# Attention's probabilities times values: one float32 product per block in place of three float16 products

## The chip, the cores and the metric

One core of a Trainium2 chip runs the kernel. The metric is device time in microseconds (us) of one execution; the time before is the median of three runs. The engines are PE (TensorE: matrix products, with its weight loads listed apart as PEld), DVE (VectorE), ACT (ScalarE), POOL (GpSimd) and SP (SyncE, which here issues all DMAs). Stationary operands are loaded by a weight load, moving operands stream past them, and sums are kept in PSUM banks.

## The reference

Three layers follow one another. Shapes: batch 4, heads 8, sequence 576, head size 64; the second layer has width 512 and 2048; the third has eight experts of 512 and 1024.

```python
scores = scale * np.matmul(q, k.transpose(0, 1, 3, 2))
scores = np.where(causal, -1e9, scores + np.minimum(bias, 0.0))   # bias from cumulated s
attn = np.exp(scores - max);  attn = attn / (sum + 1e-09)
x = np.matmul(attn, v)                       # -> (2304 tokens, 512)
h = x @ w_in;  g = h * sigmoid(1.702 * h);  x = g @ w_out
P = balanced(exp(x @ w_gate))                # eight rounds of row and column sums
out = sum_e P[:, e] * (relu(x @ w1[e]) @ w2[e])
```

## The kernel before, in words

**Stages.** Attention and the first feed-forward layer (`hp`, `acc`) are interleaved; then the last two token blocks of that layer go through in one wide pass (`accw`); then come the eight experts (`h..`, `y`). The change touches attention alone.

**The planner.** The program is put in order when it is built. `Sequencer` keeps a planned time for each engine, with rough costs per instruction (line 117). Instructions for DVE, ACT, POOL and SP are held and issued by planned time and by rank (0 goes first, then 1, 2, 3); PE's go out at once. The main loop (line 1587) asks at each step which kind of PE work is ready, in this order: V's scale, transposing finished tokens, values, transposing probabilities, scores, and last the feed-forward layer. `any_copy` (line 410) puts a copy on DVE or on ACT, whichever has the smaller planned load, `any_less` (line 417) a subtraction on POOL unless DVE is ahead by 3000 planned ns.

**Attention.** A batch and a range of queries make a group: queries 0 to 255 (two blocks of 128) or 256 to 575 (two blocks of 128 and one of 64). With 8 heads and 4 batches there are 64 entries in `heads`, and each runs as units: one unit of two query blocks, or three units of one block. That makes 128 units, and 480 blocks of 128 keys by 128 or 64 queries. A unit goes through `scores` (products into bank `sp`, mask and maximum on DVE, exponent on ACT, result `sm`), `turn` (line 791: transposes `sm` into bank `tp`, splits the result into the float16 pair `ph`, scaled by 2^15, and `pl`), `values` (line 811) and, per head, `finish` (line 833: the sum of the probabilities stands in a 65th column; DVE divides). Values of a head gather in one bank, `op`, which `finish` empties before the next head's values begin.

**V before.** The largest value of V per head is found (`find_vmax`, `find_vpow`: DMA `vr`, reduction `vmax`, a transpose `vtp`, a power of two `vw`, `vd`, a small float32 product `vbp`, copy `vpow`), V is scaled by it and split into a float16 pair (`prep_v`; both halves show as `v` in the trace; from the second batch on V comes again by DMA as `va`). A block of values is three products: `ph` by V's high half, `ph` by its low half, `pl` by its high half. `finish` takes the scale out again.

**The weights of the first layer** come as 64-bit words in 32 chunks (`conv_load`, `conv`, line 455). DVE decodes a chunk in four passes (`t`), ACT and POOL split it into a float32r pair (`wih`, `wil`, `woh`, `wol`). These have rank 2, so attention's instructions go first. Chunks from number 16 on need room that attention's first batch occupies: line 1086 waits for its last heads, and line 1066 for V of the second batch. The feed-forward layer runs over token blocks of 256; it holds two blocks at a time, starts with blocks 0 and 1 as far as weight pairs are converted, and a block's buffer comes free only when the block has gone through all eight pairs. Finished tokens of attention wait for such a buffer.

Of the kernel before, what the change touches and what calls it, by code (L numbers as in the profile page):

```python
# [23 lines left out]
PSCALE = 2.0**15  # L24
# [11 lines left out]
NEXT_V = 11  # L36
# [262 lines left out]
def kernel(  # L299
# [16 lines left out]
    BH = B * H  # L316
# [295 lines left out]

    def load_v(n):
        if n >= len(heads):
            return
        b, h, _, _, _, nkb, _ = extent(n)
        if n < 2 * H:
            h0 = h // 3 * 3
            va_of[n] = vraw[0, h // 3][:, h - h0].rearrange("p (a d) -> p a d", d=D)[:, 0:nkb]
            return  # L620
        va = apool.tile([128, nkb, D], F32, tag="va", name="va", bufs=2)
        nc.sync.dma_start(out=va, in_=vP[b, h, :, 0:nkb])
        va_of[n] = va

    v0s = [apool.tile([128, 5, D + 1], F16, name=f"v0{i}") for i in range(2)]
    v1s = [apool.tile([128, 5, D], F16, name=f"v1{i}") for i in range(2)]
    vmax = apool.tile([128, BH], F32, name="vmax")
    vpow = apool.tile([128, 2, BH], F32, name="vpow")  # L630
    ones_b = apool.tile([H, 128], F32, name="ones_b")
    vraw = {}

    def find_vmax(b, i):

        h0, h1 = 3 * i, min(H, 3 * i + 3)
        if b == 0:
            x = spool.tile([128, (h1 - h0) * 5 * D], F32, name=f"vr{i}")
        else:
            x = mpool.tile([128, (h1 - h0) * 5 * D], F32, tag="st", name="vr", bufs=2)  # L640
        x = x.rearrange("p (h a) -> p h a", h=h1 - h0)
        nc.sync.dma_start(out=x, in_=vP[b, h0:h1].rearrange("h p a d -> p h (a d)"))
        vraw[b, i] = x
        cols = slice(b * H + h0, b * H + h1)
        nc.vector.tensor_reduce(out=vmax[:, cols], in_=x, axis=AX.X, op=ALU.max, apply_absolute_value=True)

    scaled = set()

    def find_vpow(b, i0, i1):

        h0, h1 = 3 * i0, min(H, 3 * i1)
        n, cols = h1 - h0, slice(b * H + h0, b * H + h1)
        for i in range(i0, i1):
            find_vmax(b, i)
        w = apool.tile([H, 4], F32, tag="vw", name="vw", bufs=2)
        dg = apool.tile([H, 2, H], F32, tag="vd", name="vd", bufs=2)
        yield vmax
        tp = bank("T", [128, 512], "vtp")
        nc.tensor.transpose(tp[:n, 0:128], vmax[:, cols], ident)
        nc.vector.tensor_reduce(out=w[:n, 0:1], in_=tp[:n, 0:128], axis=AX.X, op=ALU.max)  # L660
        nc.vector.tensor_scalar(out=w[:n, 1:2], in0=w[:n, 0:1], scalar1=2.0**-100, scalar2=None, op0=ALU.max)
        i = w.bitcast(I32)
        nc.vector.tensor_scalar(
            out=i[:n, 2:3], in0=i[:n, 1:2], scalar1=0x7F800000, scalar2=0x7F800000,
            op0=ALU.bitwise_and, op1=ALU.bitwise_xor,
        )
        nc.vector.tensor_scalar(
            out=i[:n, 3:4], in0=i[:n, 1:2], scalar1=0x7F800000, scalar2=None, op0=ALU.bitwise_and
        )
        for m, c in ((0, 2.0**13), (1, 2.0**-14)):  # L670
            nc.vector.tensor_scalar(
                out=dg[:n, m, 0:n], in0=ident[:n, :n], scalar1=w[:n, 2 + m:3 + m], scalar2=c,
                op0=ALU.mult, op1=ALU.mult,
            )
        yield dg
        bp = bank("T", [128, 512], "vbp")[:, 0:2 * n].rearrange("p (m n) -> p m n", m=2)
        nc.tensor.matmul(bp, lhsT=ones_b[:n], rhs=dg[:n, :, 0:n], start=True, stop=True)
        nc.vector.tensor_copy(vpow[:, :, cols], bp)
        if b == 0:
            for i in range(i0, i1):  # L680
                x = vraw[b, i]
                r = vpow[:, 0, 3 * i:3 * i + x.shape[1]].rearrange("p (h o) -> p h o", o=1)
                nc.gpsimd.tensor_tensor(out=x, in0=x, in1=r.to_broadcast(list(x.shape)), op=ALU.mult)
        scaled.update((b, h) for h in range(h0, h1))

    vpows = []

    def begin_vpow(b, i0, i1, rank):
        seq.rank = rank
        g = find_vpow(b, i0, i1)  # L690
        vpows.append((g, next(g)))
        seq.rank = 0
# [12 lines left out]
    n_pv = 0  # L705
    due = []

    def more_vpow():

        if due and not any(in_mpool(c) for c in range(n_conv, n_load)):  # L710
            begin_vpow(due.pop(0), 0, 3, 1)

    def more_v():

        nonlocal n_pv
        seq.rank = 1 if n_v else 0
        while n_pv < min(len(heads), (units[n_v][0] if n_v < NU else 0) + 2):
            b, h = extent(n_pv)[0:2]
            if (b, h) not in scaled:
                break  # L720
            if n_pv not in va_of:
                load_v(n_pv)
            prep_v(n_pv)
            n_pv += 1
            load_v(n_pv)
        seq.rank = 0

    def prep_v(n):
        if n >= len(heads):
            return  # L730
        b, h, _, _, _, nkb, _ = extent(n)
        va = va_of.pop(n)
        v0, v1 = v0s[n % 2][:, 0:nkb], v1s[n % 2][:, 0:nkb]
        if n >= 2 * H:
            r = vpow[:, 0, b * H + h:b * H + h + 1]
            if seq.load("DVE") <= seq.load("ACT"):
                nc.vector.tensor_scalar(out=va, in0=va, scalar1=r, scalar2=None, op0=ALU.mult)
            else:
                nc.scalar.activation(out=va, in_=va, func=ACTF.Copy, scale=r)
        any_copy(v0[:, :, 0:D], va)  # L740
        any_less(v1, va, v0[:, :, 0:D])
        v3_of[n] = (v0, v1)
# [48 lines left out]
    def turn(i):  # L791
        sm, blocks = live[i]
        tp = bank("T", [128, 512], "tp")
        at, spots = 0, []
        for qb, rows, ke, a in blocks:
            for kb in range(qb + 1):
                nc.tensor.transpose(
                    tp[:, at:at + rows], sm[:rows, a + kb * 128:a + kb * 128 + 128], ident[:rows, :rows]
                )
                spots.append((qb, kb, rows, at))  # L800
                at += rows
        ph = apool.tile([128, 512], F16, tag="ph", name="ph", bufs=2)
        pl = apool.tile([128, 512], F16, tag="pl", name="pl", bufs=2)
        nc.scalar.activation(out=ph[:, 0:at], in_=tp[:, 0:at], func=ACTF.Copy, scale=PSCALE)
        nc.vector.scalar_tensor_tensor(
            out=pl[:, 0:at], in0=tp[:, 0:at], scalar=PSCALE, in1=ph[:, 0:at],
            op0=ALU.mult, op1=ALU.subtract,
        )
        live[i] = (ph, pl, blocks, spots)

    def values(i):
        n, u = units[i]
        qb0 = extent(n)[6][0]
        v3 = v3_of[n]
        ph, pl, blocks, spots = live.pop(i)
# [5 lines left out]
        for m, (qb, rows, ke, a) in enumerate(blocks):  # L821
            mine = [x for x in spots if x[0] == qb]
            o = op[:rows, qb - qb0, :]
            for w, (_, kb, _, at) in enumerate(mine):
                for part, nv in ((ph, 2), (pl, 1)):
                    for j in range(nv):
                        v = v3[j][:, kb, :]
                        nc.tensor.matmul(
                            o[:, 0:v.shape[1]], lhsT=part[:, at:at + rows], rhs=v,
                            start=(w == 0 and part is ph and j == 0),  # L830
                            stop=(w == len(mine) - 1 and part is pl and j == nv - 1),
                        )
    def finish(n):
# [11 lines left out]
        for _, r, c0, c1 in parts:  # L845
            nc.vector.tensor_scalar(
                out=den[:r, c0:c1], in0=op[:r, c0:c1, D], scalar1=1.0e-9 * PSCALE, scalar2=None, op0=ALU.add
# [3 lines left out]
        at = b * H + h  # L851
        for xt, r, c0, c1 in parts:
            nc.vector.scalar_tensor_tensor(
                out=xt[:r, :, h * D:(h + 1) * D], in0=op[:r, c0:c1, 0:D], scalar=vpow[:r, 1, at:at + 1],
                in1=den[:r, c0:c1].rearrange("p (a o) -> p a o", o=1).to_broadcast([r, c1 - c0, D]),
                op0=ALU.mult, op1=ALU.mult,
            )
        v3_of.pop(n)
# [45 lines left out]
    def can_value():  # L904
        if n_v >= n_t or units[n_v][0] not in v3_of:
            return never
# [3 lines left out]
        x = [live[n_v][0], live[n_v][1], *v3_of[n]]  # L910
        return max([seq.slot(ps_a, "O") if n not in outs else 0] + [seq.settled(a.tensor.name) for a in x])

    def do_value():
# [4 lines left out]
        if i in ends:  # L918
            seq.rank = 1
            n = ends[i]  # L920
            if n % (2 * H) == NEXT_V and n // (2 * H) + 1 < B:
                due.append(n // (2 * H) + 1)
            seq.rank = 0
# [139 lines left out]
    def way(c):  # L1063

        if in_mpool(c):
            if c < 4 * NP1 and (1, 0) not in vraw:
                return None, 0, 0
# [5 lines left out]
    def convert():  # L1073
# [12 lines left out]
        if c == 4 * NP0 and stage[0] is spool:  # L1086
            if n_s < NU and units[n_s][0] < 2 * H - 2 or n_v < NU and units[n_v][0] < 2 * H - 2:
                return
            if min(n_pv, n_prep) < 2 * H or spool.held() or spool2[0].held():
                return  # L1090
# [346 lines left out]
    begin_vpow(0, 0, 1, 0)  # L1437
    load_qk(2)
    nc.gpsimd.memset(ones_b, 1.0)
    for v0 in v0s:  # L1440
        nc.gpsimd.memset(v0[:, :, D:D + 1], 1.0)
# [5 lines left out]
    begin_vpow(0, 1, 3, 1)  # L1447
# [139 lines left out]
    while moe1_can is not None:  # L1587
# [3 lines left out]
        more_vpow()  # L1591
# [205 lines left out]
```

## Time and profile before

| | us |
|---|---|
| median of 3 runs | 2116.03 |
| lowest and highest | 2112.77, 2116.62 |
| profiled execution, span from first to last instruction | 2111.7 |
| PE busy | 2042.9 |
| PEld busy | 1315.4 |
| DVE busy | 1281.5 |
| ACT busy | 755.5 |
| POOL busy | 361.5 |

The profile gives the span of one execution; the median of the runs lies 4.3 us above it, which is what lies around the span and what differs between runs. Busy time is the time in which an engine has an instruction in work. Products on PE overlap, and a product's length is its way through the array; how fast products follow one another is read from their starts. The chain of waits follows the last instruction back to what released it; its shares say what the time was waiting for. Granted clock 1.00 is the upper of PE's two levels (2.4 GHz).

### The profile page before, as it was taken

How to read it: one execution, taken by the hardware profiler on the slowest of the kernel's cores; microseconds unless marked ns; L12 is line 12 of the kernel's file. 1: busy time of each engine (PE TensorE's matmuls, PEld its weight loads, DVE VectorE, ACT ScalarE, POOL GpSimd, SP SyncE). 2: the span in 40 equal slices, each digit the busy share in tenths (PEclk: the TensorE clock that was granted, in tenths of full speed). 3: DMA queues.
4: the chain of work that ended last, by engine and by line, in shares of the span. 5: the costliest groups of instructions: out<-in, count | busy, mean ns of one | idle time of the engine just before them, and what ended most of it. 6: DMA issues, size and time to landing. Idle time of an engine off the chain costs nothing.

```text
span 2111.7 us, 33686 instructions
## 1 busy us (share of the span) xinstructions
PE 2042.9 (97%) x13186; PEld 1315.4 (62%) x13186; DVE 1281.5 (61%) x2823; ACT 755.5 (36%) x1478; POOL 361.5 (17%) x363
## 2 busy tenths in 40 slices
PE   5888999999999999999999999999999999999999
PEld 3688899999987555455555555555555555555554
DVE  8999765653547754765755565565466566646333
ACT  5765564654534433312323222221232322222111
POOL 7567344443344300000000000000000000000000
PEclk9989999999999999999999999999999999999999
DMA  6354343331135642333323222123232322211220
GB/s 215 114 152 141 108 128 92 96 87 54 41 83 173 190 132 72 108 109 119 101 100 120 73 74 104 70 103 130 88 102 98 120 73 96 95 58 68 83 83 31
DMA packets 132931, 215.43 MB, mean 102 GB/s; under 512 B 14628, under 2 KB 78692, under 8 KB 132772
## 3 DMA queue, kind: packets, MB, share of 16 engines
q1 hardware_dynamic: 132772, 213.28, 31.3%
q8 instruction: 104, 1.70, 0.4%
q14 instruction: 55, 0.45, 0.1%
HBM read 190.41 MB, written 18.29 MB: 99 GB/s over the span
## 4 chain that ended last, share of the span: by engine, by line
PE 86%; DVE 8%; issue 2%; DMA 1%; ACT 1%; POOL 1%; SPq 0%; DVEq 0%; ACTq 0%; POOLq 0%
PE y L257 35%; PE hD L257 9%; PE hA L257 8%; PE hp L257 7%; PE acc L257 5%; PE hC L257 4%; PE hB L257 4%; PE hE L257 4%; DVE t L257 4%; PE sp L257 2%; PE tp L257 2%; PE op L257 2%; PE accw L257 1%; DVE sm L257 1%; DVE pl L257 1%
## 5 line engine op out<-in xcount | busy, mean ns | idle before, releaser
L257 PE MATMUL y<-w2o,h 128*128 128x512 f16 x3456 | 751.7, 379 | 0.0
L257 PEld LDWEIGHTS <-h 128*128 128x128 f16 x3456 | 337.6, 98 | 402.6
L257 PEld LDWEIGHTS <-w1o 128*128 128x128 f16 x4032 | 394.3, 98 | 268.0 <-issue 4.9
L257 DVE SCALAR_TENSOR_TENSOR acc<-y,pq,acc 128x512 f32<-128x512 f32 x126 | 94.6, 751 | 347.6 <-PE y L257 347.1
L257 PE MATMUL hD<-xt,w1o 128*128 128x384 f16 x1152 | 218.7, 326 | 3.7 <-DVE c L257 3.2
L257 PE MATMUL hA<-xt,w1o 128*128 128x384 f16 x1152 | 218.6, 326 | 0.0
L257 ACT ACTIVATE m<-hA 128x384 f32<-128x384 f32 x96 | 46.0, 480 | 408.0 <-PE hA L257 407.1
L257 PE MATMUL hp<-xh,wih 128*128 128x256 f32 (+1 forms) x512 | 154.5, 302 | 3.5 <-ACT wih L257 3.1
L257 PE MATMUL hp<-xh,wil 128*128 128x256 f32 (+1 forms) x512 | 152.3, 297 | 0.2 <-DVE wil L257 0.2
L257 PE MATMUL hp<-xl,wih 128*128 128x256 f32 (+1 forms) x512 | 152.2, 297 | 0.0
L257 ACT ACTIVATE c<-hA 128x384 f32<-128x384 f32 x96 | 47.1, 491 | 291.7 <-PE hA L257 291.5
L257 POOL TENSOR_TENSOR gl<-t,gh 128x512 fp32r<-128x512 f32 x70 | 94.1, 1345 | 163.8 <-ACT gh L257 139.8
L257 ACT ACTIVATE sm<-sm,stats 64x576 f32<-64x576 f32 (+4 forms) x160 | 93.7, 602 | 56.4 <-DVE stats L257 56.0
L257 DVE SCALAR_TENSOR_TENSOR u<-hE,u 128x384 f32<-128x384 f32 x96 | 53.5, 557 | 96.8 <-PE hE L257 96.6
L257 PE MATMUL acc<-gh,woh 128*128 128x256 f32 x384 | 111.1, 289 | 0.0
L257 PE MATMUL hE<-xt,w1o 128*128 128x384 f16 x576 | 109.4, 326 | 0.3 <-DVE sc L257 0.3
L257 PE MATMUL hB<-xt,w1o 128*128 128x384 f16 x576 | 109.3, 326 | 0.0
L257 PE MATMUL hC<-xt,w1o 128*128 128x384 f16 x576 | 109.3, 326 | 0.0
L257 PE MATMUL acc<-gl,woh 128*128 128x256 f32 x384 | 108.5, 282 | 0.0
L257 PE MATMUL acc<-gh,wol 128*128 128x256 f32 x384 | 108.3, 282 | 0.0
L257 DVE SCALAR_TENSOR_TENSOR t<-t,hp 128x512 f32<-128x512 f32 x72 | 49.1, 682 | 92.8 <-ACT t L257 92.8
L257 DVE SCALAR_TENSOR_TENSOR h<-c,h 128x384 f16<-128x384 f32 x192 | 104.1, 551 | 0.0
(199 smaller groups left out, 3343.2 us busy)
## 6 DMA issues: line engine op xcount, KB each, us to landing
xt<-xc_d SPq DMA_DIRECT2D x168, 384.0 KB
wr<-in_moe_w_dram SPq DMA_DIRECT2D x128, 256.0 KB
wm<-in_moe_w_dram SPq DMA_DIRECT2D x112, 256.0 KB
kq<-in_qk_dram SPq DMA_DIRECT2D x32, 448.0 KB
kq<-in_qk_dram SPq DMA_DIRECT2D x32, 256.0 KB
st<-in_moe_w_in_dram SPq DMA_DIRECT2D x16, 512.0 KB
st<-in_moe_w_out_dram SPq DMA_DIRECT2D x16, 512.0 KB
xc_d<-xo SPq DMA_DIRECT2D x21, 384.0 KB
```

Of the source, the lines that this page charges most:

```text
L257: self.seq.submit(self.name, what, lambda: method(*args, **named), outs, ins)
```

## The change

V of each head is loaded by one DMA straight into one of three float32 buffers with a column of ones beside it. The probabilities are copied from the bank `tp` as they are, in float32 (`pt`), and a block of values is one float32 product. The search for V's largest value, its scaling and its split go, and so do the waits for them. The diff, cut to its core:

```diff
-        ph = apool.tile([128, 512], F16, tag="ph", name="ph", bufs=2)
-        pl = apool.tile([128, 512], F16, tag="pl", name="pl", bufs=2)
-        nc.scalar.activation(out=ph[:, 0:at], in_=tp[:, 0:at], func=ACTF.Copy, scale=PSCALE)
-        nc.vector.scalar_tensor_tensor(
-            out=pl[:, 0:at], in0=tp[:, 0:at], scalar=PSCALE, in1=ph[:, 0:at],
-            op0=ALU.mult, op1=ALU.subtract,
-        )
-        live[i] = (ph, pl, blocks, spots)
+        pt = apool.tile([128, 512], F32, tag="pt", name="pt", bufs=2)
+        any_copy(pt[:, 0:at], tp[:, 0:at])
+        live[i] = (pt, blocks, spots)
...
-                for part, nv in ((ph, 2), (pl, 1)):
-                    for j in range(nv):
-                        v = v3[j][:, kb, :]
-                        nc.tensor.matmul(
-                            o[:, 0:v.shape[1]], lhsT=part[:, at:at + rows], rhs=v,
...
+                nc.tensor.matmul(
+                    o, lhsT=pt[:, at:at + rows], rhs=v[:, kb, :], start=(w == 0), stop=(w == len(mine) - 1)
+                )
...
+    vts = [apool.tile([128, 5, D + 1], F32, name=f"vt{i}") for i in range(N_V)]
     def load_v(n):
...
+        v_of[n] = vts[n % N_V][:, 0:nkb]
+        nc.sync.dma_start(out=v_of[n][:, :, 0:D], in_=vP[b, h, :, 0:nkb])
...
     def more_v():
-        while n_pv < min(len(heads), (units[n_v][0] if n_v < NU else 0) + 2):
-            b, h = extent(n_pv)[0:2]
-            if (b, h) not in scaled:
-                break
-            if n_pv not in va_of:
-                load_v(n_pv)
-            prep_v(n_pv)
+        while n_pv < min(len(heads), (units[n_v][0] if n_v < NU else 0) + N_V):
+            load_v(n_pv)
             n_pv += 1
-            load_v(n_pv)
...
-            nc.vector.scalar_tensor_tensor(
-                out=xt[:r, :, h * D:(h + 1) * D], in0=op[:r, c0:c1, 0:D], scalar=vpow[:r, 1, at:at + 1],
+            nc.vector.tensor_tensor(
+                out=xt[:r, :, h * D:(h + 1) * D], in0=op[:r, c0:c1, 0:D],
...
-            if c < 4 * NP1 and (1, 0) not in vraw:
-                return None, 0, 0
...
-            if min(n_pv, n_prep) < 2 * H or spool.held() or spool2[0].held():
+            if n_prep < 2 * H or spool.held() or spool2[0].held():
...
-    begin_vpow(0, 0, 1, 0)
-    begin_vpow(0, 1, 3, 1)
-        more_vpow()
```

`N_V` is 3; the functions `find_vmax`, `find_vpow`, `begin_vpow`, `more_vpow` and `prep_v` are removed.

## Rows read from the trace of the kernel before

**Rows 1.** Windows; columns: window, its length, busy time (instructions) per engine, clock, DMA.
```profile
0.00:125.00 125.00, 88.27 (x753) 71.41 (x754) 107.70 (x301) 80.04 (x162) 81.31 (x99) 0.92 0.54 169
125.00:235.00 110.00, 95.67 (x785) 91.02 (x784) 96.33 (x171) 61.58 (x116) 69.69 (x56) 0.95 0.39 126
...
250.00:600.00 350.00, 348.81 (x3447) 332.00 (x3447) 194.77 (x636) 185.87 (x351) 140.25 (x163) 1.00 0.28 83
...
692.00:2112.00 1420.00, 1407.19 (x7673) 737.17 (x7671) 813.20 (x1620) 380.26 (x769) 21.23 (x11) 1.00 0.29 96
```
**Rows 2.** Chain of waits, shares by line: 20 to 235 us, then 235 to 600.
```profile
by line: DVE t L257 38.3%; issue 6.7%; PE sp L257 6.6%; DVE sm L257 6.1%; PE op L257 5.0%; DVE pl L257 5.0%; PE hp L257 4.9%; PE tp L257 4.4%; DMA two<-aux_d 4.1%; ACT t L257 2.9%; PE accx L257 2.6%; DVE xg L257 2.0%; DVE stats L257 1.9%; D
...
by line: PE hp L257 31.2%; PE acc L257 30.3%; PE sp L257 10.2%; PE tp L257 9.7%; PE op L257 8.9%; issue 2.6%; PE xtp L257 1.6%; DMA kq<-in_qk_dram 0.9%; PE accx L257 0.8%; PE vbp L257 0.5%; DVE vmax L257 0.5%; POOL gl L257 0.3%; DVE sm L257
```
**Rows 3.** The tile `t`; columns: engine, operation, duration in ns (min/median/max), first and last start.
```profile
L257 DVE SCALAR_TENSOR_TENSOR t<-st,t x64: 670/699/2432, 22.2 to 230.4; 128x512 int32<-128x512 int32 x64
...
L257 ACT CAST wih<-t x16: 603/620/622, 26.2 to 223.1; 128x512 fp32r<-128x512 f32 x16
```
**Rows 4.** Groups on DVE from 20 to 235 us: busy us, mean ns, idle before.
```profile
L257 DVE SCALAR_TENSOR_TENSOR t<-st,t 128x512 int32<-128x512 int32 x64 | 63.4, 990 | 0.8
...
L257 DVE SCALAR_TENSOR_TENSOR pl<-tp,ph 128x384 f16<-128x384 f32 (+2 forms) x44 | 24.4, 562 | 1.5 <-ACT ph L257 1.4
...
L257 DVE TENSOR_REDUCE vmax<-vr 128x3 f32<-128x960 f32 (+1 forms) x3 | 3.1, 1024 | 0.0
```
**Rows 5.** Windows of the tiles `op` (PE, DVE), `pl` (PE, PEld, DVE), `v` (PE, DVE, ACT, POOL).
```profile
0.00:235.00 235.00, 27.00 (x468) 14.15 (x64) 0.93 0.47 149
235.00:600.00 365.00, 42.54 (x972) 27.38 (x128) 1.00 0.28 84
...
0.00:235.00 235.00, 22.11 (x156) 17.08 (x156) 24.97 (x45) 0.93 0.47 149
235.00:600.00 365.00, 37.16 (x324) 30.87 (x324) 46.45 (x83) 1.00 0.28 84
...
0.00:235.00 235.00, 27.00 (x468) 1.32 (x2) 9.19 (x26) 18.78 (x28) 0.93 0.47 149
```
**Rows 6.** The tile `va`: its DMAs.
```profile
L257 SPq DMA_DIRECT2D va<-in_v_dram x48: 328/442/1548, 97.3 to 540.3; - x48
```
**Rows 7.** DVE and POOL in order of time from 66.3 us: start, length.
```profile
66.37 2.43 DVE L257 SCALAR_TENSOR_TENSOR t<-st,t 128x512 int32<-128x512 int32 x1
...
66.98 1.27 POOL L257 TENSOR_TENSOR gl<-t,gh 128x512 fp32r<-128x512 f32 x1
```
**Rows 8.** PE in order of time from 62.2 us: start, length; neighbours of one kind merged.
```profile
62.29 0.22 PE L257 MATMUL op<-v,ph 128*128 128x65 f16 x2
...
62.37 0.23 PE L257 MATMUL op<-v,ph 128*128 128x65 f16 x2
...
62.53 0.19 PE L257 MATMUL op<-v,pl 128*128 128x65 f16 x1
62.65 0.33 PE L257 MATMUL tp<-ident,sm 64*128 64x64 f32 x2
```
**Rows 9.** Weight loads and products in order of time from 264.3 us.
```profile
264.32 0.29 PEld L257 LDWEIGHTS vbp<-early,ones_b 1*128 1x128 f32 x2 [0.37 <-DVE early L257]
...
264.74 0.19 PEld L257 LDWEIGHTS hp<-xl,wih 128*128 128x128 f32 x1
...
264.85 0.28 PE L257 MATMUL hp<-xl,wih 128*128 128x256 f32 x1
264.97 0.28 PE L257 MATMUL hp<-xh,wil 128*128 128x256 f32 x1
```
**Rows 10.** PE from 69.7 us, and a group of weight loads with 64 columns.
```profile
69.76 0.52 PE L257 MATMUL tp<-ident,sm 64*128 64x64 f32 x5
...
L257 PEld LDWEIGHTS sp<-one 128*64 128x64 f32 x64 | 9.1, 142 | 1.4 <-DVE stats L257 0.5
```
**Rows 11.** What SP's queue waited for, 0 to 250 us: total, times, longest.
```profile
SPq L257 <- DVE t L257: 65.0, 16, 18.5
```

More of the change, by code (lines that the diff above doesn't have):

```diff
@@ L23 @@
 F64_ZERO = 2.0**-15
-PSCALE = 2.0**15
 def f32(ap):
@@ L35 @@
 N_ONE = 3
-NEXT_V = 11
+N_V = 3
 LATENCY = {
@@ L611, in prep @@
         any_less(one[64:128, 0:nq], kq[64:128, 0:nq], f32(one[64:128, 0:nq]))
+    vts = [apool.tile([128, 5, D + 1], F32, name=f"vt{i}") for i in range(N_V)]
+    ones_b = apool.tile([H, 128], F32, name="ones_b")
+    v_of = {}
+    n_pv = 0
     def load_v(n):
-        if n >= len(heads):
-            return
         b, h, _, _, _, nkb, _ = extent(n)
[L617 to L665, printed above, removed]
-        )
[L667 to L684, printed above, removed]
@@ L686 @@
-    vpows = []
[L688 to L692, printed above, removed]
+        v_of[n] = vts[n % N_V][:, 0:nkb]
+        nc.sync.dma_start(out=v_of[n][:, :, 0:D], in_=vP[b, h, :, 0:nkb])
+    vpows = []
     def can_vpow():
@@ L703, in do_vpow @@
             vpows.insert(0, (g, x))
[L705 to L711, printed above, removed]
     def more_v():
@@ L716, in more_v @@
         seq.rank = 1 if n_v else 0
-        while n_pv < min(len(heads), (units[n_v][0] if n_v < NU else 0) + 2):
-            b, h = extent(n_pv)[0:2]
-            if (b, h) not in scaled:
-                break
-            if n_pv not in va_of:
-                load_v(n_pv)
-            prep_v(n_pv)
+        while n_pv < min(len(heads), (units[n_v][0] if n_v < NU else 0) + N_V):
+            load_v(n_pv)
             n_pv += 1
-            load_v(n_pv)
         seq.rank = 0
[L728 to L742, printed above, removed]
     def scores(i):
@@ L813, in values @@
         qb0 = extent(n)[6][0]
-        v3 = v3_of[n]
-        ph, pl, blocks, spots = live.pop(i)
+        v = v_of[n]
+        pt, blocks, spots = live.pop(i)
         if u[0] == qb0:
@@ L824, in values @@
             for w, (_, kb, _, at) in enumerate(mine):
-                for part, nv in ((ph, 2), (pl, 1)):
-                    for j in range(nv):
-                        v = v3[j][:, kb, :]
-                        nc.tensor.matmul(
-                            o[:, 0:v.shape[1]], lhsT=part[:, at:at + rows], rhs=v,
-                            start=(w == 0 and part is ph and j == 0),
-                            stop=(w == len(mine) - 1 and part is pl and j == nv - 1),
-                        )
+                nc.tensor.matmul(
+                    o, lhsT=pt[:, at:at + rows], rhs=v[:, kb, :], start=(w == 0), stop=(w == len(mine) - 1)
+                )
     def finish(n):
@@ L846, in finish @@
             nc.vector.tensor_scalar(
-                out=den[:r, c0:c1], in0=op[:r, c0:c1, D], scalar1=1.0e-9 * PSCALE, scalar2=None, op0=ALU.add
+                out=den[:r, c0:c1], in0=op[:r, c0:c1, D], scalar1=1.0e-9, scalar2=None, op0=ALU.add
             )
@@ L850, in finish @@
         nc.vector.reciprocal(out=den[:, 0:c], in_=den[:, 0:c])
-        at = b * H + h
         for xt, r, c0, c1 in parts:
-            nc.vector.scalar_tensor_tensor(
-                out=xt[:r, :, h * D:(h + 1) * D], in0=op[:r, c0:c1, 0:D], scalar=vpow[:r, 1, at:at + 1],
+            nc.vector.tensor_tensor(
+                out=xt[:r, :, h * D:(h + 1) * D], in0=op[:r, c0:c1, 0:D],
                 in1=den[:r, c0:c1].rearrange("p (a o) -> p a o", o=1).to_broadcast([r, c1 - c0, D]),
-                op0=ALU.mult, op1=ALU.mult,
+                op=ALU.mult,
             )
-        v3_of.pop(n)
+        v_of.pop(n)
         if h < H - 1:
@@ L904, in can_value @@
     def can_value():
-        if n_v >= n_t or units[n_v][0] not in v3_of:
+        if n_v >= n_t or units[n_v][0] not in v_of:
             return never
@@ L909, in can_value @@
             return never
-        x = [live[n_v][0], live[n_v][1], *v3_of[n]]
+        x = [live[n_v][0], v_of[n]]
         return max([seq.slot(ps_a, "O") if n not in outs else 0] + [seq.settled(a.tensor.name) for a in x])
@@ L917, in do_value @@
         values(i)
[L918 to L923, printed above, removed]
     def try_finish():
@@ L1436 @@
     sums()
-    begin_vpow(0, 0, 1, 0)
     load_qk(2)
     nc.gpsimd.memset(ones_b, 1.0)
-    for v0 in v0s:
-        nc.gpsimd.memset(v0[:, :, D:D + 1], 1.0)
+    for vt in vts:
+        nc.gpsimd.memset(vt[:, :, D:D + 1], 1.0)
     seq.rank = 1
```

1 line of the change is left out of this document (removed).

## The prediction

> **What bounds the kernel now.** I first cut the span by work [rows 1]. Attention and the first feed-forward layer fill 0 to 600 us, the wide pass of that layer 600 to 692, the eight experts the rest. PE is busy in 1407 of the last 1420 us, and nothing the change touches runs there. The change acts inside the first 600 us, which have two parts. From 250 to 600 us PE is busy 348.8 of 350 us while DVE has 194.8. Before 235 us PE is busy 184 of 235 and DVE 204 (107.7 + 96.3), the fullest engine.
>
> The chains of waits say the same [rows 2]. From 20 to 235 us `DVE t` leads with 38.3%: `t` is the decoding and splitting of the first layer's weights, 32 chunks, the last of which ends at about 232 us (the last `t` of that kind starts at 230.4 [rows 3]). I call this the weight stage. From 235 to 600 us the chain is PE almost alone (`hp`, `acc`, `sp`, `tp`, `op`: 90%): the PE stage. So one edit has two prices: DVE time counts before 235 us, PE time after it.
>
> The weight stage must end when the 32 chunks are converted, because the first token blocks need all of their weight pairs, the token buffers hold two blocks, and attention can run only about one group of heads ahead of them.
>
> **What it removes.** *DVE.* The residue `pl` runs 128 times, 24.4 us in 20 to 235 us [rows 4] and 71.4 us in all [rows 5]; it goes. `vmax`, 3.1 us there, goes too: 27.5 us. The scalings, casts and power-of-two steps of V on DVE are small in this window and put at 3 to 4 us: 31 in all. The same steps before 20 us fall into a start that waits for POOL and DMAs; they are counted at nothing.
>
> *ACT and POOL.* `ph` (one ACT pass per unit) becomes the copy `pt` of the same size from PSUM, chosen between DVE and ACT by planned load. In the weight stage DVE is the fuller one and the same choice gave ACT all 16 casts to `wih` [rows 3], so I put it on ACT: no change there. Before 235 us ACT loses V's casts, 9.2 us, and POOL V's subtractions, 18.8 us [rows 5]. Neither engine is the bound. POOL matters in another way: `t<-st,t` takes 0.70 us in the median and up to 2.43 [rows 3], and the 2.43 us one, at 66.37, ends only after a POOL subtraction that ran beside it from 66.98 to 68.25 [rows 7]. Fewer POOL instructions mean fewer such waits: the mean of 64 is 990 ns [rows 4], so about 19 us of stretch; POOL loses 18.8 of its 151 us, an eighth, so I estimate 2 us here and up to 5 with the other forms of `t`.
>
> *PE.* Five `vtp`/`vbp` pairs go; in the PE stage `vbp` and the reduction `vmax` before it are 0.5% of the chain each [rows 2]: about 2 us.
>
> **What it adds on PE.** A block is one 128-key square of probabilities times 65 columns; there are 480 (1440 float16 products in three parts [rows 5]), 320 with 128 rows of queries and 160 with 64. Three float16 products begin at 62.29, and the next block's at 62.37; the last product of three blocks begins at 62.53, eight steps later, so 0.03 us each and 0.09 a block [rows 8]. A float32 product is not in the trace in this shape, but small ones are: `vbp`, one `matmul` in the code, shows as two weight loads and two products; the two loads together take 0.29 us, and a load of that kind is 0.19 long (that of `hp` at 264.74), so the second begins 0.10 us after the first, though the product between them has two columns [rows 9]. The `hp` products, with the same kind of load and 256 columns, follow one another every 0.12 us (264.85, 264.97). A float32 weight load of 128 columns thus paces its product at 0.10 to 0.12 us; I take 0.11. The moving side is cheaper: five float32 transposes of 64 columns take 0.52 us [rows 10], less a last one of at most 0.24, so 0.06 to 0.07 each. So a 128-row block becomes 2 x 0.11 = 0.22 us. For a 64-row block the load has half the columns (142 ns long for `sp` [rows 10]), and the moving side decides: 2 x 0.06 = 0.12 to 0.13.
>
> Something is given back: after a run of values the next instruction needs a 128-column float32 load behind a very short product; the transpose starts 0.12 us after the last `op` (62.53 to 62.65) where 0.03 is the rhythm [rows 8]. In the new rhythm that load is no exception. That is 0.09 us for each of 128 units, 11.5 us.
>
> Sum: 320 x 0.13 = 41.6, 160 x 0.03 = 4.8, less 11.5: 35 us. Of the 1440 products 468 lie before 235 us and 972 after [rows 5], so 24 us fall into the PE stage, on the path one for one, since nothing else runs on PE while a product does; less 2 us for `vtp`/`vbp`: +22. The other 11 us fall into the weight stage, into PE's 51 idle us. Bounds for the PE stage: without the 11.5 given back 24 + 8 = 32; with 64-row blocks at 0.22 as well, 160 x 0.09 x 0.68 = 10 more; below, if the moving side is hidden so that 64-row blocks cost what they do now, 19. I take 22, between the `vbp` and the `hp` row.
>
> **What the weight stage gives back.** Lower bound from the chain: `DVE pl` is 5.0% of its 215 us, 10.8 us, while `PE op`, also 5.0%, grows by 11 us over its present 18.7 (156 blocks x 0.09 and gaps between units of 0.1), +6.4: 4 us. Upper bound: DVE is 87% busy, attention's work goes first and the conversion takes what is left, so every us freed moves the conversion forward: 31 + 5 = 36. From about 174 to 235 us there is little attention left to remove, and PE comes nearer to its limit, so not all is used. I take 25, 0.8 x 31, because the DVE rows are the direct ones.
>
> **Edits at nothing.** V comes by one DMA per head, 64 where there were 48 [rows 6] and, three a batch, 12; fewer bytes in all, in runs of 256 bytes, and the core's DMA share is 0.47 and 0.28 in the two stages [rows 5]. They stand on SP's one queue with `kq`, `st` and the `aux` rows, and each now waits for the products of the head three before, where the old ones waited for a buffer of V's scaling: if PE is late, `kq` and `st` behind it wait too. What covers this: SP waited 65 us for `DVE t` in 0 to 250 us already [rows 11], so it stands idle for the converters and not for room. Uncovered, I put it at what the nearest small load, `two<-aux_d`, holds of the chain now: 4.1% of 215 us, 9 us [rows 2]. The loads of chunks 16 and 17 and the second weight place no longer wait for V; those loads were issued long before use. The last step of a head multiplies without the scalar: same shape. The wait `PE op <- DVE pl` goes and `PE op` waits for `pt` instead, 0.5 us sooner a unit; PE in its own stage waits for almost nothing.
>
> **Sum.** 2111.7 - 25 + 22 = 2109 for the profiled span, that is -3. The median shown is 2116.0, 4.3 above the span (the three runs lie from 2112.8 to 2116.6), so 2113. A measurement here can tell about 0.2%, 4 us.
>
> **Rivals.**
> (1) *DVE's relief comes through whole.* For it: DVE's 87%, the stretch under POOL. Against: PE gets 11 us more work in a stage where it is not idle by much. -36 + 22 = -14: 2102.
> (2) *Slower: the float32 weight loads become the bound of the weight stage too.* Attention's chain there goes score, exponent, transpose, values, finish on PE, and the O bank holds one head; if values at 2.4 times their length hold up the finishing of heads, the freed DVE time stays idle and only the 4 us of the chain come back, while the PE stage pays 22 to 30. It decides wherever the stage gives back less than the PE stage takes, 22 us. For it: `PE op` and `PE tp` on the chain before 235 us. With 4 us back and 22 to 30 paid it is +18 to +26; with some of DVE's time back after all, from +4 on: 2131 in the middle.
> (3) *Weight loads don't hide behind products.* Then a 128-row block is 2 x (0.11 + 0.06) = 0.34 and a 64-row one 2 x (0.06 + 0.06) = 0.24: 320 x 0.25 + 160 x 0.15 = 104 us, 70 of them in the PE stage; with 25 - 15 back, about +60: 2176. Against it: the `hp` products of [rows 9], which follow one another every 0.12 us with a load of 0.19 us each. The Trainium skill, "TensorE: Matmul & The Clock Gate", Part 3, "The mechanism", says that a weight load overlaps a running product only where the row groups differ; here all use all rows, so by that rule this rival would hold, and the `hp` rows speak against it.
>
> **How the numbers follow.** Forecast 0.40 (own range -13 to +7), rival (1) 0.28, (2) 0.25, (3) 0.07. Faster by over 0.2%: all of (1) and 0.17 of the forecast, 0.45. Within 0.2%: 0.19 of the forecast and 0.03 of (2), 0.22. Slower: 0.04 + 0.22 + 0.07 = 0.33. The range leaves out (3) and the ends of the others: 2095 to 2137.
>
> **What would show it.** In the trace after: two loads and two products per block, 960 in all, 0.11 us apart for 128 rows and 0.06 for 64; `op` and its neighbours growing by 22 us between the end of the weight stage and the wide pass; the last `woh` cast near 206 us in place of 231; `pt` mostly on ACT; no `DVE pl`; the last 1420 us unchanged. I am wrong on the mechanism if the conversion ends later than 225 us, if PE shows idle time behind V's loads, or if 128-row blocks take 0.3 us.

## The result and the profile after

The changed kernel takes 2134.1 us (median of 4 runs, 2131.4 to 2134.9) against 2114.4 us for the kernel before (4 runs, 2111.4 to 2116.6): ratio 1.0092, 95% interval 1.0078 to 1.0105. It is 19.7 us slower where 3 us faster was forecast. The profiled execution has a span of 2129.6 us (2111.7 before).

Windows of the changed kernel, with the columns of [rows 1]:

```profile
0.00:125.00 125.00, 95.71 (x641) 85.01 (x642) 91.34 (x253) 76.95 (x145) 70.26 (x80) 0.99 0.55 165
125.00:235.00 110.00, 97.85 (x766) 93.98 (x766) 93.58 (x172) 55.46 (x100) 55.81 (x47) 0.97 0.49 156
250.00:600.00 350.00, 349.96 (x2963) 337.33 (x2963) 148.94 (x520) 138.75 (x244) 115.23 (x126) 1.00 0.23 63
710.00:2130.00 1420.00, 1408.46 (x7682) 737.94 (x7679) 814.86 (x1621) 381.71 (x771) 21.26 (x11) 1.00 0.29 96
```

DVE (third busy time) has 16.4 us less in the first window and 2.8 less in the second; PE is as full as before from 250 us on, and the last 1420 us are unchanged. The granted clock is not what makes it slower: its mean is higher than before in the first two windows (0.99 and 0.97 for 0.92 and 0.95) and 1.00 in the third, as before. Three instants cut the rest. The last cast to `woh` ends the conversion (**C**). The sixteenth `xg` on DVE finishes the sixteenth head, and with it the tokens of token block 1 are whole (**H**). The cast `xo<-accx` on ACT starts when block 1, the second of the two that run while weights arrive, leaves PE (**B**); the weight stage is over then. Each instant is the last start, or for B the first, in a row of a tile. The changed kernel:

```profile
L256 ACT CAST woh<-t x16: 605/622/628, 40.1 to 206.6; 128x512 fp32r<-128x512 f32 x16
L256 DVE TENSOR_TENSOR xg<-op,stats x16: 277/288/292, 19.8 to 117.1; 128x128 f32<-128x128 f32 x16
L256 ACT ACTIVATE xo<-accx x2: 577/578/578, 244.5 to 245.0; 128x512 f32<-128x512 f32 x2
```

The kernel before, in the same order:

```profile
L257 ACT CAST woh<-t x16: 612/618/625, 42.6 to 231.1; 128x512 fp32r<-128x512 f32 x16
L257 DVE SCALAR_TENSOR_TENSOR xg<-op,vpow,stats x16: 332/340/351, 27.1 to 115.7; 128x128 f32<-128x128 f32 x16
L257 ACT ACTIVATE xo<-accx x2: 579/588/597, 247.3 to 248.3; 128x512 f32<-128x512 f32 x2
```

The conversion ends 24.5 us earlier (231.1 to 206.6), as forecast; block 1 leaves only 2.8 us earlier (247.3 to 244.5). From B to the start of the last two outputs (`xo<-acc`) before the wide pass, the trace has 370.7 us where it had 348.2: the PE stage is 22.5 us longer. Together that is 19.7 us at the end of the PE stage (615.2 for 595.5). What follows is 1.8 us shorter in these two executions, whose spans are 17.9 us apart; that the medians too differ by 19.7 is chance.

The chain of waits from 235 to 600 us has `op` at 17.1%, where it had 8.9% [rows 2]:

```profile
by line: PE hp L256 30.1%; PE acc L256 29.3%; PE op L256 17.1%; PE sp L256 10.9%; PE tp L256 10.1%; PE xtp L256 1.4%; PE accx L256 0.8%; PE vbp L256 0.3%; PE vtp L256 0.1%; issue 0.0%
```

Where the conversion's lead went shows in the chain of waits from 206 to 250 us, the changed kernel first (DVE 3%, PE nearly all: the converted weights lie ready and PE works them off), the kernel before second (DVE's `t` still leads):

```profile
by line: PE hp L256 39.9%; PE accx L256 27.4%; PE op L256 8.3%; PE acc L256 7.0%; PE sp L256 4.7%; PE tp L256 4.3%; PE xtp L256 3.7%; DVE t L256 3.0%; PE vbp L256 1.4%; PE vtp L256 0.5%; issue 0.4%
```
```profile
by line: DVE t L257 29.0%; PE hp L257 24.5%; PE accx L257 13.5%; PE acc L257 7.0%; ACT t L257 4.6%; PE xtp L257 4.1%; PE op L257 3.5%; issue 3.4%; PE tp L257 3.2%; DVE wil L257 3.2%; PE sp L257 2.3%; ACT woh L257 1.5%; ACT wih L257 1.4%; AC
```

And in the windows between H and B, the kernel before first, the changed one second: PE has 114 of 129 us and 112 of 126. So with the conversion out of the way, and PE's work in it as it is, some 12 to 15 us were left to come out of this stretch (an estimate from PE's idle time there).

```profile
118.00:247.00 129.00, 114.26 (x962) 108.68 (x962) 110.47 (x209) 72.70 (x138) 76.99 (x65) 0.96 0.40 129
```
```profile
118.00:244.00 126.00, 111.75 (x881) 106.75 (x880) 104.02 (x207) 62.39 (x114) 62.57 (x53) 0.97 0.44 140
```

PE in order of time from 90 us in the changed kernel, its loads below, and the groups of `op` and `pt`:

```profile
90.21 1.75 PE L256 MATMUL op<-vt,pt 128*128 128x65 f32 x14 [0.53 <-DVE xgl L256]
91.89 0.52 PE L256 MATMUL tp<-ident,sm 64*128 64x64 f32 x5
...
90.18 1.64 PEld L256 LDWEIGHTS op<-vt,pt 128*128 128x128 f32 x14 [0.71 <-issue]
...
L256 PEld LDWEIGHTS op<-vt,pt x960: 132/192/338, 17.8 to 577.3; 128*128 128x128 f32 x128, 128*64 128x64 f32 x64
...
L256 ACT COPY pt<-tp x90: 403/479/589, 17.3 to 574.5; 128x384 f32<-128x384 f32 x48, 128x512 f32<-128x512 f32 x24, 128x320 f32<-128x320 f32 x18
L256 DVE COPY pt<-tp x38: 479/557/692, 127.1 to 574.0; 128x384 f32<-128x384 f32 x16, 128x320 f32<-128x320 f32 x14, 128x512 f32<-128x512 f32 x8
```

480 blocks give 960 loads and products; 14 of them (seven blocks) take 1.68 us until the transpose starts. Single starts lie 112 ns apart with 128 rows (median) and 57 to 61 with 64. The window of tile `op` has 42.70 us of PE before 235 us and 70.88 after (27.00 and 42.54 before the change [rows 5]):

```profile
0.00:235.00 235.00, 42.70 (x312) 0.98 0.52 161
235.00:600.00 365.00, 70.88 (x648) 1.00 0.24 64
```

### The profile page after: what moved, and what is told of

The parts are those of the page before. It is cut to its first block, busy times and chain, and to the rows that moved or that the text cites. A ratio compares the mean times of both kernels' runs of the same rounds, so it can differ in the third digit from the quotient of the medians.

```text
span 2129.6 us, 32342 instructions
## 1 busy us (share of the span) xinstructions
PE 2073.2 (97%) x12691; PEld 1355.3 (64%) x12691; DVE 1219.6 (57%) x2672; ACT 702.4 (33%) x1341; POOL 312.8 (15%) x298
## 4 chain that ended last, share of the span: by engine, by line
PE 89%; DVE 7%; issue 2%; POOL 1%; DMA 1%; ACT 1%; SPq 0%; ACTq 0%; DVEq 0%; POOLq 0%
PE y L256 35%; PE hD L256 9%; PE hA L256 8%; PE hp L256 7%; PE acc L256 6%; PE hC L256 4%; PE hB L256 4%; PE hE L256 4%; PE op L256 4%; DVE t L256 4%; PE sp L256 2%; PE tp L256 2%; PE accw L256 1%; DVE sm L256 1%; PE accx L256 1%
## 5 line engine op out<-in xcount | busy, mean ns | idle before, releaser
L256 PE MATMUL hA<-xt,w1o 128*128 128x384 f16 x1152 | 218.6, 326 | 0.0
L256 ACT ACTIVATE m<-hA 128x384 f32<-128x384 f32 x96 | 46.1, 480 | 409.3 <-PE hA L256 408.2
L256 PE MATMUL op<-vt,pt 128*128 128x65 f32 (+1 forms) x960 | 113.6, 265 | 9.2 <-ACT pt L256 4.2
L256 PEld LDWEIGHTS op<-vt,pt 128*128 128x128 f32 (+1 forms) x960 | 104.8, 181 | 20.2 <-ACT pt L256 6.6
L256 PE MATMUL acc<-gh,woh 128*128 128x256 f32 x384 | 110.8, 289 | 0.0
```

Source lines behind the costliest of these rows:

```text
L256: self.seq.submit(self.name, what, lambda: method(*args, **named), outs, ins)
```

## The experiments

All were run beside the kernel before. The table gives time, ratio with its 95% interval, the three instants, and the PE stage from B to the last output before the wide pass; instants and stage are of one profiled execution each. The executions of one kernel differ by up to 8 us, and the profiled one can lie at either end (e17: 2127.2 of 2127.2 to 2134.2; e9: 2113.6 of 2107.3 to 2113.6), so B of two rows is not compared to the microsecond. "Short" means two of three feed-forward products in the first two token blocks, "no floor" one DVE step less per converted chunk, "hold" a conversion held back, "order" another planned order of the same work.

| kernel | us | ratio | C | H | B | B-C | B-H | PE stage |
|---|---|---|---|---|---|---|---|---|
| before | 2114.4 | 1 | 231.1 | 115.7 | 247.3 | 16.2 | 131.6 | 348.2 |
| after | 2134.1 | 1.0092 (1.0078-1.0105) | 206.6 | 117.1 | 244.5 | 37.9 | 127.4 | 370.7 |
| e1 three bf16 | 2106.0 | 0.9954 (0.9938-0.9971) | 204.9 | 115.2 | 242.6 | 37.7 | 127.4 | 347.7 |
| e2 bf16, first 24 heads | 2130.2 | 1.0072 (1.0057-1.0087) | 203.1 | 113.4 | 241.8 | 38.7 | 128.4 | 371.3 |
| e3 DVE pass | 2148.1 | 1.0157 (1.0142-1.0173) | 228.3 | 130.8 | 259.6 | 31.3 | 128.8 | 370.9 |
| e4 planner's price | 2134.0 | 1.0092 (1.0076-1.0107) | 200.2 | 121.5 | 249.3 | 49.1 | 127.8 | 370.3 |
| e5 after, short | 2117.9 | 1.0013 (1.0004-1.0023) | 217.1 | 112.0 | 235.1 | 18.0 | 123.1 | 366.8 |
| e6 before, short | 2112.5 | 0.9991 (0.9982-1.0001) | 229.8 | 110.1 | 245.3 | 15.5 | 135.2 | 347.7 |
| e7 after, hold | 2139.2 | 1.0115 (1.0100-1.0130) | 225.5 | 117.8 | 248.4 | 22.9 | 130.6 | 371.0 |
| e8 e1, hold | 2106.6 | 0.9960 (0.9945-0.9975) | 218.6 | 110.0 | 240.4 | 21.8 | 130.4 | 345.9 |
| e9 before, no floor | 2111.1 | 0.9980 (0.9971-0.9990) | 217.1 | 121.8 | 248.9 | 31.8 | 127.1 | 348.5 |
| e10 after, no floor | 2118.7 | 1.0024 (1.0015-1.0033) | 188.0 | 110.8 | 234.3 | 46.3 | 123.5 | 368.3 |
| e11 after, both cuts | 2105.8 | 0.9959 (0.9943-0.9974) | 197.2 | 108.7 | 217.2 | 20.0 | 108.5 | 371.3 |
| e12 one bf16 | 2073.0 | 0.9799 (0.9782-0.9816) | 213.2 | 100.4 | 230.1 | 16.9 | 129.7 | 326.5 |
| e13 before, both cuts | 2099.9 | 0.9934 (0.9915-0.9953) | 223.8 | 111.1 | 236.6 | 12.8 | 125.5 | 346.8 |
| e14 e1, short | 2084.0 | 0.9862 (0.9846-0.9878) | 208.4 | 104.4 | 224.7 | 16.3 | 120.3 | 343.8 |
| e15 e1, no floor | 2086.1 | 0.9876 (0.9860-0.9893) | 178.5 | 102.7 | 224.6 | 46.1 | 121.9 | 343.8 |
| e16 before, order | 2111.6 | 0.9992 (0.9983-1.0002) | 228.8 | 108.7 | 245.2 | 16.4 | 136.5 | 345.5 |
| e17 after, order | 2133.4 | 1.0087 (1.0072-1.0103) | 202.4 | 111.8 | 239.7 | 37.3 | 127.9 | 371.1 |
| e18 e9, order | 2098.6 | 0.9934 (0.9917-0.9950) | 208.6 | 107.9 | 230.6 | 22.0 | 122.7 | 346.9 |

**The product alone (e1, e2, e12).** The probabilities go to PE as bf16, and the values as the upper halves of their float32 words; e1 issues that product three times, e2 does so in the first 24 heads alone, e12 issues it once.

```
+        if <this head>: pt = pt.bitcast(BF16)
...
+                    for j in range(3):
+                        nc.tensor.matmul(o, lhsT=pt[...], rhs=v.bitcast(BF16)[:, kb, 1::2], ...)
```

> The changed kernel with its product alone at the old price: P is copied to bfloat16, V is read as the upper halves of its float32 words, and a block is the same 16-bit product three times over (the sum of the probabilities is tripled with it, so the quotient stands, at bfloat16 accuracy); the planner is told the price it had for one float32 product, so the order is that of the changed kernel. Theory A (the relief on DVE is lost because PE's longer products fill the weight stage): the second token block ends near 226 us instead of 244.5, the stage after it lasts as long as before the change (349 us), and the whole is 2092 us, some 22 under the kernel before. Rival B (the order of work in the changed kernel, made by a planner that prices the product at half, holds the weight stage): the second block still ends at 240 to 245 us and only the PE stage gets its 22 us back: 2112.

> The same, but only for the 24 heads whose values fall into the weight stage; the other 40 have the float32 product. Theory A: the weight stage ends near 226 to 228 us, the PE stage keeps its 22 us: 2115. Rival B: the stage ends at 240 to 245 us as in the changed kernel: 2131 to 2134.

> One bf16 product per block (probabilities rounded to bf16, values cut to the upper half of their word) in place of three equal ones: 960 products of about 0.03 us fewer. If products are on the path one for one where PE is saturated (972 of 1440 lie there): the PE stage falls by 18 to 22 us, the weight stage by 0 to 4, time 2081 to 2089 from 2106. If PE in that stage waits for other engines as soon as it has less work: 2095 to 2104.

e1 has the change's relief of DVE and the product time of before: the PE stage is 347.7 us again, 23.0 less than in the changed kernel, so all of the 22.5 us is the float32 product. The windows of that stage, the changed kernel first, then e1, have PE full in both:

```profile
244.00:615.00 371.00, 370.96 (x3134) 357.23 (x3133) 155.49 (x536) 145.99 (x257) 120.46 (x131) 1.00 0.23 63
```
```profile
242.00:590.00 348.00, 347.18 (x3446) 330.53 (x3445) 154.31 (x536) 145.92 (x257) 120.84 (x131) 1.00 0.25 68
```

But block 1 leaves at 242.6, only 4.7 us sooner than before, though the conversion ends 26 us sooner: the instant that theory B forecast, though not by its cause (e4 below). The time, 2106.0, lies 6 us under its figure and 14 over theory A's. In e2 the weight stage gains 2.7 us (244.5 to 241.8): the longer product costs next to nothing there. e12 did better than expected: 21.2 us less in the PE stage, as forecast (648 products of 0.033 us), and 12.5 in the weight stage, where 0 to 4 were; there H is 14.8 us earlier. Its PE is full all the same:

```profile
230.00:556.00 326.00, 326.00 (x2813) 310.62 (x2813) 155.83 (x552) 145.50 (x259) 120.79 (x131) 1.00 0.29 79
```

So e1 and e12 beat both kernels, e12 by 2.0%, at the price of holding both factors of this product in bf16 (the probabilities rounded, the values cut off to the upper halves of their words).

**DVE's time in the changed kernel (e3), and the planner (e4).** e3 puts a residue pass back on DVE whose result nobody reads; e4 prices the float32 product as two loads and two products.

```
+        nc.vector.scalar_tensor_tensor(out=pl[:, 0:at], in0=tp[:, 0:at], scalar=1.0, in1=pt[:, 0:at], ...)
...
+            if ins[0].dtype == F32:
+                return 2 * max(self.size(ins[0]) / 1.2 + 5, 2 * n / 2.4 + 4)
```

> The changed kernel with one more DVE pass per unit, of the size and place of the old residue pass, whose result nobody reads: 71 us of DVE in all, 25 in the weight stage. Theory A: PE's work sets the end of the weight stage, so the conversion ends later (near 225 us instead of 207) and the second block only a little later (244 to 250): 2134 to 2140. Rival C (DVE sets the end and what ate its relief is something else): the second block ends 15 to 20 us later, 2150.

> The changed kernel with the planner's price of a float32 product set to what the trace shows, 0.22 us for 128 rows and 0.12 for 64, in place of 0.11. Theory A: PE has the same work, so within 5 us of the changed kernel, 2129 to 2139. Rival B: the order improves and 8 to 20 us come back: 2114 to 2126.

The time and B of e3 are those of rival C, not of theory A: DVE's relief is worth something, and without it the changed kernel loses another 14 us. But B is 31.3 us behind C there, so it is not the conversion that held it; what moved with B is H, from 117.1 to 130.8:

```profile
L256 DVE TENSOR_TENSOR xg<-op,stats x16: 269/280/285, 23.1 to 130.8; 128x128 f32<-128x128 f32 x16
```

A true price gave nothing (e4): a different order, and the same time. Rival B of e1, the planner's low price, is refuted with it.

**PE's work behind the sixteenth head (e5, e6).** In both, the first two token blocks have two of three products.

```
+                if j < 2 and n == 1:
+                    continue
```

> The changed kernel with two of the three products of each feed-forward block of the first two token blocks (the third is left out, so those blocks are less exact): about 31 us less for PE between 50 and 245 us, DVE, ACT and POOL as they were. In every run so far block 1 was written out 127 to 130 us after its tokens were whole (115 to 131 us), whenever the conversion ended. Theory T (PE's own work behind those tokens ends the weight stage, so converted weights wait for PE): block 1 ends near 216 in place of 244.5, right behind the conversion at 207; the time is 2104 to 2112. Rival R (something else that was not touched, the order of attention or DVE, ends the stage): PE only idles more, block 1 ends after 232 and the time is above 2120.

> The same cut in the kernel before (31 us less for PE in the first two token blocks). Theory T: here the conversion, which ends at 231, is right behind PE, so the cut gives only about 7 us (block 1 at 239 to 242, time 2105 to 2110), and the changed kernel with the cut comes out level with this one: DVE's relief is worth its 20 us once PE has room. Rival R: the cut gives the same in both kernels, and the changed one stays about 20 us slower than this one.

The cut gives the changed kernel 16 us and the kernel before 1.5: the difference that theory T is about, though neither lies in its range (2104 to 2112 and 2105 to 2110), and the two end 5.4 us apart and not level. Without the cut the changed kernel needs another 37.9 us when the conversion ends, with it 18.0; in the kernel before it is 16.2 and 15.5, which I read as the time that the last pair of weights takes to go through. So PE ends the weight stage of the one and the conversion that of the other. Two things took from the gain of e5. The conversion itself ended 10 us later. And the cut is smaller than the 31 us of its products: from 118 us to B the mean granted clock is 0.87 in e5 and 0.82 in e6, where the uncut kernels had 0.97 and 0.96, so the products that are left take longer. The windows, e5 first, then e6:

```profile
118.00:235.00 117.00, 97.35 (x691) 91.40 (x691) 94.22 (x188) 65.66 (x118) 66.69 (x56) 0.87 0.42 131
```
```profile
118.00:245.00 127.00, 97.47 (x709) 88.01 (x709) 109.78 (x205) 69.11 (x130) 71.64 (x62) 0.82 0.41 130
```

PE is idle for 29.5 us of this stretch in e6, and block 1 still leaves right behind the conversion: it is not PE that ends the stage there.

**Holding the conversion back (e7, e8).**

```
+        if c >= 10 and n_fin < 2 * H:
+            return
```

> The changed kernel, with the conversion held at 10 of 32 chunks until the first 16 heads are finished (before the change it had done 10 or 11 by then, after it 14). Theory T1 (the DVE time that was freed went to conversion, which nobody waits for at 118 us, in place of the attention that makes block 1's tokens): tokens whole at 104 to 110, block 1 at 230 to 237, time 2119 to 2126. Rival T2 (the attention of the first 16 heads is bound by its own chain of score, exponent, transpose and product): tokens stay at 114 to 118, conversion ends later, time 2130 to 2145.

> The kernel with three bf16 products per block in place of one float32 product (2106.0 alone) with the same hold of the conversion at 10 chunks until 16 heads are finished. T1: tokens at 102 to 108, time 2091 to 2098. T2: tokens stay at 113 to 117, time 2104 to 2118.

The conversion stands still for 32 us (the tenth and eleventh of its casts on ACT, to `wih` or `woh`, start at 90.1 and 121.9 us in e7), and H stays at 117.8. That the freed DVE time had merely gone to the wrong work (T1) is refuted for the changed kernel; in e8 H comes 5 us earlier, between the two forecasts, but the conversion ends 14 us later, and B gains 2.2 us, the time nothing.

**DVE's work, cut (e9 to e11, e13 to e15).** One of DVE's five steps per chunk is left out; e11 and e13 have the cut of e5 as well, e14 is e1 with that cut.

```
-            nc.vector.tensor_scalar(out=f32(t), in0=f32(t), scalar1=F64_ZERO, scalar2=None, op0=ALU.max)
```

> The kernel before without one of the five DVE steps of each converted chunk (the floor for tiny weights is left out, so weights at or near zero come out wrong): DVE loses 32 passes of 0.39 us or more, about 20 us with their stretch under POOL, and nothing else changes. Theory K (kink: DVE's conversion ends the weight stage of this kernel, but PE's own work stands only 3 to 5 us behind it): conversion ends 15 to 20 us earlier, block 1 is out only 3 to 6 us earlier, time 2108 to 2112. Rival C (DVE's relief comes through): block 1 out 13 to 18 us earlier, time 2095 to 2101.

> The same step left out in the changed kernel. K: conversion ends 15 to 20 us earlier still (186 to 192), block 1 stays within 3 us of 244.5, time 2130 to 2136. C: time 2114 to 2121.

> The same step left out in the changed kernel that has a third fewer products in the first two token blocks (2117.9 alone). K: PE has 31 us more room here, so DVE's relief does come through: 2101 to 2108. If DVE's relief is never worth anything in the changed kernel: 2115 to 2120.

> The kernel before with both cuts: a third fewer products in the first two token blocks (31 us of PE) and no floor step in the conversion (about 20 us of DVE); each of them alone gave 1.5 and 3.4 us here. Theory W (two walls: PE's and DVE's work in the weight stage are level in this kernel, so only both together shorten it): 2094 to 2101, conversion and block 1 both 12 to 20 us earlier. Rival A (a third thing ends the stage, the cuts just add): 2107 to 2112.

> The kernel with DVE's relief and three bf16 products per block (2106.0 alone), with a third fewer products in the first two token blocks. W: DVE is already 31 us lighter, so PE is the wall that is left, and its cut gives 12 to 17 us: 2089 to 2095. A: 2102 to 2106.

> The same kernel (2106.0 alone) without the floor step instead. W: DVE is not the wall any more, so more relief gives 0 to 5 us: 2101 to 2106. If DVE's time counts here as it does in the changed kernel (15 us for this step): 2090 to 2095.

The kink of e9's expectation held for the time of e9 (3.4 us; its block 1 leaves no earlier) and for e11 (2105.8), and failed for e10 (15) and e15 (20): the conversion is not what ends these two, B-C is 46 us, yet they gain, and H comes 6 and 12 us earlier in them. H in e10, and C in e15:

```profile
L256 DVE TENSOR_TENSOR xg<-op,stats x16: 272/290/293, 19.8 to 110.8; 128x128 f32<-128x128 f32 x16
```
```profile
L259 ACT CAST woh<-t x16: 617/620/622, 35.4 to 178.5; 128x512 fp32r<-128x512 f32 x16
```

e13 came out at theory W's time, with C 7 us and B 11 us earlier where 12 to 20 were forecast. The cut of e14 gave 22 us, more than W's 12 to 17, and e15 is against W. What W leaves out is H, which moves in e14 and e15 too. That DVE's steps delay the sixteenth head is not shown by it: without the floor step H is earlier in e10 and e15, 6.1 us later in e9, and the same in e18 as in e16 (107.9 and 108.7).

**The order alone (e16 to e18).** Same instructions, other order:

```
-            return 70 + n / (1.92 if quick else 0.96)
+            return 80 + n / (1.92 if quick else 0.96)
```

> The kernel before, same instructions, but the planner prices each DVE instruction 10 ns higher, so the order across engines comes out a little different. If order alone is worth little: 2110 to 2118. If it is worth as much as the effects in question: off by 8 us or more.

> The changed kernel, same instructions, with the planner's DVE price 10 ns higher. If order alone is worth little: 2130 to 2138, and the change costs 16 to 24 us whatever the order. If not: off by 8 us or more.

> The kernel before without the floor step (2111.1), with the planner's DVE price 10 ns higher. If DVE's relief is really worth nothing in this kernel: 2107 to 2115. If the first order was merely an unlucky one: 2095 to 2103.

The loss of the change stands: 2133.4 against 2111.6 in the new order. But e18 is 12.5 us faster than e9 with the same work, so e9's small gain was an unlucky order: in the order of e16 the kernel before gains 13 us from DVE's relief. So the 14 and 15 us of e3 and e10, one order each, stand little above what order alone did here. H in e9, then in e18, and B in both:

```profile
L257 DVE SCALAR_TENSOR_TENSOR xg<-op,vpow,stats x16: 329/344/353, 27.7 to 121.8; 128x128 f32<-128x128 f32 x16
...
L257 ACT ACTIVATE xo<-accx x2: 575/586/597, 248.9 to 249.4; 128x512 f32<-128x512 f32 x2
```
```profile
L257 DVE SCALAR_TENSOR_TENSOR xg<-op,vpow,stats x16: 331/342/351, 26.1 to 107.9; 128x128 f32<-128x128 f32 x16
...
L257 ACT ACTIVATE xo<-accx x2: 597/598/598, 230.6 to 233.5; 128x512 f32<-128x512 f32 x2
```

**What the table says as a whole.** The weight stage has two walls, and the later one counts. With whole products, B is the later of C + 16 and H + 127, within some 5 us in all 15 rows: before, 247 and 243; after, 223 and 244. With the short products all five rows lie within 4 us of C + 16, so none of them shows where their wall behind H stands; e11 has the least, 108.5 us. The two constants are fitted to this table and not tested beyond it. That the wall behind H is PE's own work shows in two ways: behind C PE is nearly all of the chain of the changed kernel, and where the conversion is early with and without the cut, the cut of PE's products shortens B-H by 15 us (e10 to e11, 123.5 to 108.5) and by 7 (e1 to e14).

## Why the prediction was wrong

- *The PE stage pays 22 us*: right, in part by luck. It pays 22.5; e1 takes them away with the product alone. The paces were right (0.11 and 0.06 forecast, 0.112 and 0.057 to 0.061 measured), so rival (3), 0.34 us a block, did not happen: loads hide behind the products. The rule of the Trainium skill ("TensorE: Matmul & The Clock Gate", Part 3, "The mechanism"), that a weight load overlaps a running product only where the row groups differ, would have it otherwise; all these loads use all rows, and the 1.68 us for 14 products, with loads of 0.19 us, decide against it. The term that was off is what was to be given back behind a run of values, 0.09 us a unit. From the last `op` to the start of a transpose the PE stage has 0.124 us before and 0.153 after (medians), beside paces of 0.03 and 0.112, so the wait behind a run shrank by only about 0.05. Counted from each start to the next start on PE, `op` takes 60.5 us of that stage where it took 34.0: 26.5 more, not 24. That `vtp`, `vbp` and the other products took 4 us less there, where 2 were forecast, made up for it.
- *The conversion ends 25 us earlier*: right, 24.5 (206.6 where 206 was forecast).
- *"The weight stage must end when the 32 chunks are converted"*: this step failed, and with it the term of 25 us, which measured 2.8. In the kernel before, by the two constants above, the conversion was the later wall by 4 us only (9 in the order of e16). Behind it stood PE, which needed 127 us after the sixteenth head, and that head did not come sooner (117.1 for 115.7; 121.5 and 111.8 in the orders of e4 and e17). The rows held the warning: from 125 to 235 us PE has 95.7 us and DVE 96.3 [rows 1], two engines level, but I added this window to the one ahead of it and read the sum, 184 against 204, as DVE's bound. From H to B it is PE that is fuller, 114 us to 110. The chain's 38% for `DVE t` could not show it: a chain names what came last, not how close the next one stood.
- *PE's 11 us more in the weight stage fall into its idle time*: nearly right. e2 gets back 2.7 us of them.
- *Rival (2)* had the right sign, a near time (2131) and a near term for the weight stage (4 us), by luck, for a reason that e2 speaks against: taking the float32 products out of the weight stage gives 2.7 us. What holds that stage is the feed-forward products behind the sixteenth head, which the change does not touch.
- *DVE loses 31 us there*: its busy time before 235 us fell by 19. The listed steps are gone; 7.3 us of the difference are reductions of the experts' weights (`early`, seven where there was one), which begin when the conversion is over.
- *The rest*: 90 of 128 copies `pt` on ACT, no `DVE pl`, and the last 1420 us as they were, as said. No wait of `op` ended with V's loads: the edits at nothing cost nothing that the trace shows.

**Open:** what sets H. It is 14.8 us earlier with a shorter product (e12), 13.7 later with more work on DVE (e3), 6.3 earlier with less (e10); but order alone moves it as well (before and e16: 115.7 and 108.7; after, e4 and e17: 117.1, 121.5 and 111.8, with the same work), so these moves are not shown to be the product's or DVE's. Holding the conversion does not move it in the changed kernel. The attention of the first 16 heads passes through all engines, and no one of them was shown to set its pace. Why the relief of e1 did not bring H forward, while the smaller one of e15 on top of it gave 12 us, is therefore not settled; an unlucky order is possible, as in e9.

## What to carry to other kernels

Where two engines are both near full in a stage, price the relief of one by the distance to the other's wall, and cut the windows at the points where the work's supply changes (here where the second block's tokens are whole), not over the whole stage. Replacing three 16-bit products by one float32 product pays only where PE has room: each 128-row block became 0.13 us longer, and in a stage in which PE is full all of that is on the path. When a planner writes the order, try the same work in a second order before explaining a difference of 10 us.

## What the runs showed of the hardware

- A float32 product of 128 x 65 with a 128-column load is issued as two loads and two products, 112 ns apart, with loads of 0.19 us each; with 64 columns 57 to 61 ns. The loads overlap the products before them.
- A bf16 product whose moving side is read with a stride (every second half-word of a float32 tile) nearly keeps the 0.03 us pace of the float16 one: in e1 the starts of the products of 128-row blocks are 34 ns apart in the median (30 in the kernel before), and its PE stage is as long as that of the kernel before (347.7 and 348.2 us).
- Less work for PE can come with a lower clock: with a third of the feed-forward products of two token blocks left out, the mean granted clock from 118 us to B fell from 0.97 to 0.87 (e5) and from 0.96 to 0.82 (e6), and PE was busy 97 us in both, for 112 and 114.
